# A recurrence and two dense layers on one core: chunk outputs as four products side by side with tokens on the partitions, turned by four transposes

## The chip, the cores and the metric

The kernel runs on one core of a Trainium2 chip. The metric is the device time of one launch in microseconds. An execution was profiled apart; its trace has every instruction of the five engines (PE is TensorE, DVE is VectorE, ACT is ScalarE, POOL is GpSimd, SP is SyncE) and the DMA packets.

## The reference

For 4 batches of 8 heads, each with a state of 40 x 40 numbers and 768 tokens, the attention part runs a recurrence; the result, 3072 tokens of 320 numbers, goes through two dense layers. All is in 32-bit floating point.

```python
for t in range(S):
    y[:, :, t] = np.einsum('bhd,bhde->bhe', rt, state)
    Sa = np.einsum('bhde,bhe->bhd', state, at)
    state_decay = state * wt[:, :, None, :] - np.einsum('bhd,bhe->bhde', Sa, bt)
    state = state_decay + np.einsum('bhd,bhe->bhde', vt, kt)
...
h = x @ w_in                      # 320 -> 1024
solu = h * softmax(h)
ln = (solu - mean) / sqrt(var + 1e-06) * g_ln
x = ln @ w_out                    # 1024 -> 320
...
h = x @ w_in                      # 320 -> 2048
g = np.maximum(h, 0.0) + alpha * np.minimum(h, 0.0)
out = g @ w_out                   # 2048 -> 320
```

## The kernel before

The 768 tokens are cut into 12 windows of 64 tokens, each of two chunks of 32, so there are 24 chunks. The 32 heads stand as 16 slots `s` times two groups `e`; a tile holds group 1 on its lower partitions and group 0 from partition 64 on. Within a chunk the recurrence is turned into matrix products and a triangular inverse; from chunk to chunk only the state goes on.

Chunk g has a time slot of its own, `slot(g)`, which records the stages of the recurrence in this order: `stage_x(g)` (tile `px`), `stage_uf(g-1)` (`pf`), `stage_u(g)` (`pu`), `stage_g2(g-1)` (`pg`, scores of a token against the chunk's tokens, masked by VectorE into `YS`), `stage_st(g)` (`pst`, the new state), `stage_y(g-1)` (`py`, the outputs of the chunk before), and `stage_s(g)` (`pss`, the state turned). Between them `side` puts transposes `pt` of coming windows (`trans`), products `pg` of `gen1`, and parts of the inverse (`pv`, `pn`). Into every gap the planner lets products of the first dense layers flow from a queue: `h` (line 803), `ptr`, `po` (line 877), `ptx`. After the last chunk come the last layers, `ph` (line 1324) and `acc` (lines 1342 to 1344).

The order on each engine is not written by hand: `note`, `pace`, `until` and `run` carry on a time of the planner's own, with a cost in microseconds for each step, and choose from it what stands next. Where the queue has nothing to give and the planner counts too few columns of late, `pop` puts a filler, a product of zeros called `zero` (line 313), or `busy` (line 358) in the first four slots. So other costs in one stage move instructions in every slot behind it.

The recurrence's products take their PSUM banks in turn from a ring of four (`bank`). A bank comes free when the engine that reads it is done (`ring[bk] = t + LAT`), and the fifth request waits for the first.

`stage_y` before: `blank(py)` (line 660) writes zeros into partitions 32 to 63 of the whole bank, 512 columns in bf16; then for each slot two products put 40 rows of `py` at partition 0 and 40 at partition 64, features on the partitions and 32 tokens on the free axis (line 750). VectorE multiplies all 104 partitions with H, the running product of the decays, into `Y` (line 756). Behind the second chunk of a window `x_move` sends `Y` to DRAM (`xd`), `x_load` brings it back, `x_split` makes `xt` of it (lines 784 to 788), and the first-layer products read that.

Of the kernel before, what the change touches and what calls it, by code (L numbers as in the profile page):

```python
# [18 lines left out]
D = 40  # L19
# [26 lines left out]
def tile_kernel(ctx: ExitStack, tc: tile.TileContext, w_fm, a0_fm, a_fm, kb_fm, r_fm, v_fm, v_tm,  # L46
# [66 lines left out]
    LMN = [lm.tile([128, 32, 32], F32, name=f"LMN{i}") for i in range(3)]  # L113
    VUS = [ca.tile([128, 2, 4, 2, 80], F32, name=f"VUS{i}") for i in range(2)]
    VUF = [ca.tile([120, 16, 2, 32], F32, name=f"VUF{i}") for i in range(2)]
    YS = [ca.tile([128, 2, 16, 32], F32, name=f"YS{i}") for i in range(2)]

    def f32(ap):
# [17 lines left out]
    def init():  # L136
        for t, c, k in ((GR, 0, 0), (VR, 0, 1), (LMN[2], 16, 2)):
            i = tri[:, 256 + 16 * k:272 + 16 * k].unsqueeze(1).to_broadcast([128, 32, 16])
            nc.gpsimd.tensor_copy(out=t[:, :, c:c + 16], in_=i)
        for t in YS:  # L140
            nc.gpsimd.memset(t[32:64, 1], 0.0)
            nc.gpsimd.memset(t[0:64, 0], 0.0)
            nc.gpsimd.memset(t[64:128, 1], 0.0)
        for t in VUS:
            nc.gpsimd.memset(t[32:64, 0], 0.0)
            nc.gpsimd.memset(t[32:64, 1], 0.0)
        for t in VUF:
            nc.gpsimd.memset(t[32:64], 0.0)
        for t in KBS:
            nc.gpsimd.memset(t[32:64, 0], 0.0)  # L150
            nc.gpsimd.memset(t[96:128, 1, 0], 0.0)
        for t, i in ((VUS[0], 0), (KBS[0], 1)):
            nc.gpsimd.memset(t[64:128, i], 0.0)
            nc.gpsimd.memset(t[0:32, 1 - i], 0.0)
        nc.gpsimd.memset(ebias, -float(896 << 23))
        nc.gpsimd.memset(half, -0.5)
        nc.gpsimd.memset(tiny, 1e-12)
        nc.gpsimd.memset(one, 1.0)
# [116 lines left out]
    def bank(shape, name):  # L275

        if not plain():
            until(lambda: ring[-4] if len(ring) > 3 else 0.0)
        ring.append(INF)
        return ps_at.tile(shape, F32, name=name, tag="at"), len(ring) - 1  # L280
# [79 lines left out]
    def flush(n):  # L360
        while len(queue) > n:
            if head():
                pop()
            else:
                until(queue[0][3])
# [289 lines left out]
            put(("U", g, pe))(t + LAT)  # L655
        ring[bk] = t + LAT

    def blank(p):

        nc.tensor.matmul(p[32:64].rearrange("p s t -> p (s t)"), lhsT=D1[:, 1:17].bitcast(BF16),  # L660
                         rhs=D1[:, 0:16 * p.shape[1]].bitcast(BF16), start=True, stop=True)
        note(0.11 * p.shape[1] / 8, 8 * p.shape[1], 1)

    def stage_uf(g):
        v, vuf = VUS[g % 2], VUF[g % 2]
        until(("U", g, 0), ("U", g, 1))
# [74 lines left out]
    def stage_y(g):  # L741
        w, c = divmod(g, 2)
        k, y = KBS[g % 4], YS[g % 2]
        until(("ys", g, 0), ("ys", g, 1), ("kb", g), ("ks", g))
        py, bk = bank([128, 16, 32], "py")
        blank(py)
        for s in range(16):
            for e, o in EO:
                K = 128 if e else 104 + s // 8 * 16
                nc.tensor.matmul(py[o:o + D, s, :], lhsT=k[0:K, 1 - e, s, :], rhs=y[0:K, e, s, :], start=True, stop=True)  # L750
            pace(0.08, 128, 4)
        ts = slice(c * 32, c * 32 + 32)
        if c == 0:
            st["Y"] = m1.tile([104, 16, 64], F32, name="Y")
        Y = st["Y"]
        t = run("V", 0.7, lambda: nc.vector.tensor_tensor(out=Y[:, :, ts], in0=py[0:104], in1=st[w]["H"][:, :, ts], op=ALU.mult),
                now[0] + PL)
        ring[bk] = t + LAT
        put(("yt", g))(t)
        if c and g < NG - 1:  # L760
            later(t, lambda: x_move(w))
# [398 lines left out]
    def slot(g):  # L1160
        st["slot"] = g
        fin = g == NG - 1
        queue.extend(mlp_tasks(g))
        box.setdefault("h", 0.0)
        nd = (ND if g < 4 else NL if g >= NG - 4 else NC)[g % 4]

        def due(n):
            lane["due"] += n
        if g + 1 < NG:
            load_v(g + 1)  # L1170
        stage_x(g)
        slot_tasks(g)
        side(g, "a")
        if g:
            stage_uf(g - 1)
        side(g, "b")
        stage_u(g)
        if g:
            stage_g2(g - 1, 0)
            stage_g2(g - 1, 1)  # L1180
        side(g, "c")
        due((nd + 3) // 4)
        if not fin:
            stage_st(g, 0)
            stage_st(g, 1)
        side(g, "x")
        due((nd + 1) // 4)
        if g == NG - 2:
            early_w()
        if g:  # L1190
            stage_y(g - 1)
        if g + 1 < NG:
            load_r(g + 1)
        side(g, "d")
        due((nd + 2) // 4)
        if not fin:
            stage_s(g)
        side(g, "e")
        due(nd // 4)
        side(g, "f")  # L1200
        flush(RES if g >= DEEP else MOST)
        side(g, "z")
        if fin:
            stage_uf(g)
            stage_g2(g, 0)
            stage_g2(g, 1)
            stage_y(g)
        flush(0 if fin else KQ if g >= DEEP else MOST)

    def phase1():  # L1210
# [484 lines left out]
```

## Time and profile before

| | |
|---|---|
| median of 3 runs | 1022.45 us (1016.11 to 1030.37) |
| profiled execution | 1025.12 us |
| its span, first to last instruction | 1023.1 us |
| mean granted clock of TensorE | 0.958 |
| busy: PE, DVE, ACT, POOL | 957.8, 658.2, 545.3, 302.4 us |

The span is what the trace covers; the execution's own time has 2.0 us around it. A busy PE is not a PE at its peak, since matmuls are pipelined and their ends are modelled: what a stage takes is best read from its first start to the first start of the stage behind it.

### The profile page before, as it was taken

Reading aid. Unit: us, or ns where it says so; the run is one execution under the profiler, and the core shown is the slowest. Engines: PE = TensorE matmul, PEld = TensorE weight load, DVE = VectorE, ACT = ScalarE, POOL = GpSimd, SP = SyncE. Lnnn points to the kernel's source line nnn. Section 1 sums busy time; section 2 is a strip of 40 time slices with the busy share of each in tenths; the row PEclk is TensorE's granted clock in tenths of the full one; section 3 lists DMA queues with packets and bytes.
Section 4 is the critical chain, followed back from the end, with each engine's and each line's share of the span. In section 5 each row is a group of like instructions: output and inputs, shape, how many; then the busy total and the mean of one; then the engine's idle time right before and its main releaser. Section 6 shows DMA issues by size and latency. Waiting matters only on the chain.

```text
span 1023.1 us, 34881 instructions
## 1 busy us (share of the span) xinstructions
PE 957.8 (94%) x15018; PEld 765.1 (75%) x15018; DVE 658.2 (64%) x1214; ACT 545.3 (53%) x1276; POOL 302.4 (30%) x352
## 2 busy tenths in 40 slices
PE   7789998999999999989999999899999999999996
PEld 3456566676677776767777767788989898989896
DVE  8797987688868886888864564634444445334443
ACT  1375657486768784858777785992121212212121
POOL 8500210113221221332121142623333333334332
PEclk8798977899899997999999999999999999999999
DMA  7634424333543353344353444442020100101010
GB/s 187 186 90 120 121 80 119 91 96 102 141 114 97 80 148 91 96 125 137 101 154 106 110 121 149 147 124 71 1 52 1 39 13 12 29 1 26 1 27 17
DMA packets 101532, 90.09 MB, mean 88 GB/s; under 512 B 52284, under 2 KB 76092, under 8 KB 101372
## 3 DMA queue, kind: packets, MB, share of 16 engines
q1 hardware_dynamic: 101372, 87.80, 31.1%
q8 instruction: 120, 1.97, 0.8%
q14 instruction: 40, 0.33, 0.1%
HBM read 70.20 MB, written 17.56 MB: 86 GB/s over the span
## 4 chain that ended last, share of the span: by engine, by line
PE 72%; ACT 12%; DVE 9%; issue 4%; DMA 1%; SPq 0%; POOL 0%; DVEq 0%; ACTq 0%; POOLq 0%
PE ph L1324 16%; PE po L877 9%; PE h L803 7%; PE acc L1342 5%; PE acc L1343 5%; PE acc L1344 5%; PE py L750 3%; PE pst L686 3%; ACT KBS L597 3%; PE pg L727 2%; PE pf L671 2%; PE pu L648 2%; PE pg L501 1%; PE zero L313 1%; PE pn L562 1%
## 5 line engine op out<-in xcount | busy, mean ns | idle before, releaser
L1331 POOL TENSOR_TENSOR gll<-gt,gh 128x512 fp32r<-128x512 f32 (+1 forms) x112 | 129.1, 1154 | 228.2 <-ACT gh L1330 222.3
L1330 ACT CAST gh<-gt 128x512 fp32r<-128x512 f32 (+1 forms) x112 | 62.5, 559 | 246.1 <-DVE gt L843 215.1
L842 DVE TENSOR_SCALAR gt<-ph,al 128x512 f32<-128x512 f32 (+1 forms) x112 | 75.4, 674 | 181.9 <-PE ph L1324 181.8
L877 PE MATMUL po<-wo,ln 128*128 128x320 f32 x384 | 131.1, 481 | 8.3 <-ACT ln L869 6.3
L877 PEld LDWEIGHTS po<-wo,ln 128*128 128x128 f32 x384 | 73.4, 204 | 36.3 <-ACT ln L869 7.1
L803 PE MATMUL h<-w1h,xt 128*128 128x512 f32 x240 | 90.2, 431 | 0.1
L1342 PE MATMUL acc<-w2h,gh 128*128 128x320 f32 x288 | 88.8, 308 | 0.0
L1343 PE MATMUL acc<-w2l,gh 128*128 128x320 f32 x288 | 88.8, 308 | 0.0
L1344 PE MATMUL acc<-w2h,gll 128*128 128x320 f32 x288 | 88.7, 308 | 0.0
L843 DVE SCALAR_TENSOR_TENSOR gt<-ph,gt 128x512 f32<-128x512 f32 (+1 forms) x112 | 68.6, 614 | 3.6
L735 DVE TENSOR_TENSOR YS<-pg,mask 64x256 f32<-64x256 f32 x96 | 40.4, 421 | 46.4 <-PE pg L727 44.7
L597 ACT COPY KBS<-pt 64x160 f32<-64x160 f32 x192 | 55.1, 287 | 18.4 <-PE pt L593 15.9
L803 PE MATMUL h<-w1l,xt 128*128 128x512 f32 x144 | 62.2, 432 | 0.2 <-POOL w1l L983 0.2
L822 POOL TENSOR_TENSOR sm<-sm,const 128x1 f32<-128x1 f32 x24 | 16.9, 704 | 151.4 <-ACT sm L819 141.0
L948 POOL TENSOR_TENSOR raw<-em 128x512 f32<-128x512 f32 (+1 forms) x28 | 36.0, 1292 | 85.7 <-issue 42.5
L1324 PE MATMUL ph<-w1h,w2h 128*128 128x512 f32 x180 | 59.3, 394 | 0.0
L358 PE MATMUL busy<-busy 128*128 128x512 bf16 x198 | 54.2, 422 | 1.3 <-POOL busy L1212 1.3
L1343 PEld LDWEIGHTS acc<-w2l,gh 128*128 128x128 f32 x288 | 54.1, 188 | 1.4
L1342 PEld LDWEIGHTS acc<-w2h,gh 128*128 128x128 f32 x288 | 54.1, 188 | 1.3
L1344 PEld LDWEIGHTS acc<-w2h,gll 128*128 128x128 f32 x288 | 54.1, 188 | 0.0
L512 ACT ACTIVATE GR<-pg 32x256 f32<-32x256 f32 x96 | 36.1, 376 | 31.2 <-PE pg L501 29.8
L712 ACT COPY KBS<-pss 40x320 f32<-40x320 f32 x92 | 38.7, 421 | 24.7 <-PE pss L709 23.4
(198 smaller groups left out, 2270.5 us busy)
## 6 DMA issues: line engine op xcount, KB each, us to landing
kbf<-in_kb_fm_dram SPq DMA_DIRECT2D x96, 96.0 KB
raw<-in_w_in_dram SPq DMA_DIRECT2D x14, 512.0 KB
raw<-in_w_out_dram SPq DMA_DIRECT2D x13, 512.0 KB
YS<-in_r_fm_dram SPq DMA_DIRECT2D x48, 112.0 KB
VUF<-in_v_fm_dram SPq DMA_DIRECT2D x48, 112.0 KB
wt<-in_w_fm_dram SPq DMA_DIRECT2D x24, 211.7 KB
VUS<-in_v_tm_dram SPq DMA_DIRECT2D x48, 80.0 KB
wr<-in_w_dram SPq DMA_DIRECT2D x8, 480.0 KB
```

The lines of the kernel that those rows point to most:

```text
L358: nc.tensor.matmul(st["busy"], lhsT=busy[:, 0:128], rhs=busy, start=True, stop=True)
L597: t = run("A", 0.29, lambda k=k, c=c, r=r, o=o: nc.scalar.copy(out=k[r:r + 64, 1 - r // 64, q * 4:q * 4 + 4, :], in_=pt[64 * c:64 * c + 64 ...
L803: nc.tensor.matmul(st["h"][:, ns], lhsT=l, rhs=r, start=j == 0, stop=j == len(ops) - 1)
L842: nc.vector.tensor_scalar(out=tmp, in0=h, scalar1=0.0, scalar2=al, op0=ALU.min, op1=ALU.mult)
L843: nc.vector.scalar_tensor_tensor(out=o, in0=h, scalar=0.0, in1=tmp, op0=ALU.max, op1=ALU.add)
L877: nc.tensor.matmul(po, lhsT=st["ln", t][:, piece], rhs=wo1[:, piece], start=piece == 0, stop=piece == K1 - 1)
L1324: nc.tensor.matmul(p, lhsT=l, rhs=r, start=j == 0, stop=j == len(ops) - 1)
L1330: nc.scalar.copy(out=gh, in_=t)
L1331: nc.gpsimd.tensor_tensor(out=gll, in0=t, in1=f32(gh), op=ALU.subtract)
L1342: nc.tensor.matmul(acc, lhsT=gh[:, cs], rhs=oh, start=f == 0, stop=False)
L1343: nc.tensor.matmul(acc, lhsT=gh[:, cs], rhs=ol, start=False, stop=False)
L1344: nc.tensor.matmul(acc, lhsT=gll[:, cs], rhs=oh, start=False, stop=f == K2 - 1)
```

## The change

The outputs are made the other way round: `YS` is the stationary operand (32 tokens) and the keys `KBS` the moving one (40 features). Four slots stand side by side on the 32-partition quarters of one bank, so that no partition is left unwritten, and the blanking product goes. ScalarE copies `py` into a new tile `YP`, whose features 40 to 63 were set to zero once at the start. A new stage, `stage_yt`, turns `YP` with four transposes into another bank of the ring, in the shape that `py` had before, and the product with H follows as it was. `stage_yt(g-1)` is recorded behind `stage_s(g)`, and for the last chunk right behind `stage_y`. The planner's cost of the products is 8 steps of 0.08 us in place of 16 and the blank; the transposes have 0.1 us each.

```diff
--- before.py
+++ after.py
@@ -113,6 +113,7 @@
     LMN = [lm.tile([128, 32, 32], F32, name=f"LMN{i}") for i in range(3)]
     VUS = [ca.tile([128, 2, 4, 2, 80], F32, name=f"VUS{i}") for i in range(2)]
     VUF = [ca.tile([120, 16, 2, 32], F32, name=f"VUF{i}") for i in range(2)]
+    YP = ca.tile([128, 4, 2, 64], F32, name="YP")
     YS = [ca.tile([128, 2, 16, 32], F32, name=f"YS{i}") for i in range(2)]
 
     def f32(ap):
@@ -137,6 +138,7 @@
         for t, c, k in ((GR, 0, 0), (VR, 0, 1), (LMN[2], 16, 2)):
             i = tri[:, 256 + 16 * k:272 + 16 * k].unsqueeze(1).to_broadcast([128, 32, 16])
             nc.gpsimd.tensor_copy(out=t[:, :, c:c + 16], in_=i)
+        nc.gpsimd.memset(YP, 0.0)
         for t in YS:
             nc.gpsimd.memset(t[32:64, 1], 0.0)
             nc.gpsimd.memset(t[0:64, 0], 0.0)
@@ -655,12 +657,6 @@
             put(("U", g, pe))(t + LAT)
         ring[bk] = t + LAT
 
-    def blank(p):
-
-        nc.tensor.matmul(p[32:64].rearrange("p s t -> p (s t)"), lhsT=D1[:, 1:17].bitcast(BF16),
-                         rhs=D1[:, 0:16 * p.shape[1]].bitcast(BF16), start=True, stop=True)
-        note(0.11 * p.shape[1] / 8, 8 * p.shape[1], 1)
-
     def stage_uf(g):
         v, vuf = VUS[g % 2], VUF[g % 2]
         until(("U", g, 0), ("U", g, 1))
@@ -742,13 +738,27 @@
         w, c = divmod(g, 2)
         k, y = KBS[g % 4], YS[g % 2]
         until(("ys", g, 0), ("ys", g, 1), ("kb", g), ("ks", g))
-        py, bk = bank([128, 16, 32], "py")
-        blank(py)
-        for s in range(16):
-            for e, o in EO:
-                K = 128 if e else 104 + s // 8 * 16
-                nc.tensor.matmul(py[o:o + D, s, :], lhsT=k[0:K, 1 - e, s, :], rhs=y[0:K, e, s, :], start=True, stop=True)
-            pace(0.08, 128, 4)
+        py, bk = bank([128, 4, 2, 40], "py")
+        for n in range(4):
+            for e in range(2):
+                for q in range(4):
+                    s = 4 * n + q
+                    K = 128 if e else 104 + s // 8 * 16
+                    nc.tensor.matmul(py[q * 32:q * 32 + 32, n, 1 - e, :], lhsT=y[0:K, e, s, :], rhs=k[0:K, 1 - e, s, :],
+                                     start=True, stop=True)
+                pace(0.08, 150, 8)
+        t = run("A", 0.43, lambda: nc.scalar.copy(out=YP[:, :, :, 0:D], in_=py), now[0] + PL)
+        ring[bk] = t + LAT
+        put(("YP", g))(t + LAT)
+
+    def stage_yt(g):
+        w, c = divmod(g, 2)
+        until(("YP", g))
+        py, bk = bank([128, 16, 32], "pyt")
+        for n in range(4):
+            nc.tensor.transpose(py[0:104, 4 * n:4 * n + 4, :].rearrange("p s t -> p (s t)"),
+                                YP[:, n].rearrange("p e d -> p (e d)")[:, 0:104], ident)
+            pace(0.1, 256, 1)
         ts = slice(c * 32, c * 32 + 32)
         if c == 0:
             st["Y"] = m1.tile([104, 16, 64], F32, name="Y")
@@ -1195,6 +1205,8 @@
         due((nd + 2) // 4)
         if not fin:
             stage_s(g)
+        if g:
+            stage_yt(g - 1)
         side(g, "e")
         due(nd // 4)
         side(g, "f")
@@ -1205,6 +1217,7 @@
             stage_g2(g, 0)
             stage_g2(g, 1)
             stage_y(g)
+            stage_yt(g)
         flush(0 if fin else KQ if g >= DEEP else MOST)
 
     def phase1():
```

In the order below, `L` numbers of the changed kernel are its own: 747 is the new output product, 759 the new transpose, 750 the new copy; `pss` is line 705, `pt` 595, `h` 813, `po` 887, `ptx` 901 there.

TensorE around the output of chunk 15, the second chunk of its window, before:

```order
L803 MATMUL h<-w1l,xt 128x512
L803 MATMUL h<-w1h,xt 128x512
L686 MATMUL pst<-VUS_170,KBS_158 40x40 x2
L660 LDWEIGHTS D_150
L660 MATMUL py<-D_150 32x512
L750 MATMUL py<-YS_175,KBS_161 40x32 x32
L593 MATMUL pt<-ident,kbf 128x104 x8
L709 MATMUL pss<-ident,VUS_171 120x40 x16
L593 MATMUL pt<-ident,kbf 128x104 x4
L803 MATMUL h<-w1h,xt 128x512
```

and now:

```order
L901 MATMUL ptx<-ident,xs 64x128
L813 MATMUL h<-w1h,xt 128x512
L747 MATMUL py<-KBS_161,YS_176 32x40 x32
L595 MATMUL pt<-ident,kbf 128x104 x8
L705 MATMUL pss<-ident,VUS_171 120x40 x16
L813 MATMUL h<-w1l,xt 128x512
L759 MATMUL pyt<-ident,YP 104x128 x4
L813 MATMUL h<-w1h,xt 128x512 x2
L813 MATMUL h<-w1l,xt 128x512
L595 MATMUL pt<-ident,kbf 128x104 x8
L813 MATMUL h<-w1h,xt 128x512
```

The blank is gone, a first-layer product stands between `pss` and the transposes, and the transposes stand between the two halves of the `pt` work.

ScalarE at the same chunk, from the copies of `ptx` to the copies of the turned state, before:

```order
L896 COPY x_7908<-ptx 64x128
L597 COPY KBS_160<-pt 64x160 x2
L597 COPY KBS_161<-pt 64x160 x2
L931 ACTIVATE em<-em,const 128x256
L932 ACTIVATE em<-em 128x256
L597 COPY KBS_160<-pt 64x160 x2
L597 COPY KBS_161<-pt 64x160 x2
L712 COPY KBS_159<-pss 40x320
L712 COPY KBS_159<-pss 56x320
L712 COPY KBS_159<-pss 40x320
L712 COPY KBS_159<-pss 56x320
```

and now:

```order
L906 COPY x_8002<-ptx 64x128
L849 ACTIVATE P<-P,sm 128x1024
L750 COPY YP<-py 128x8x40
L599 COPY KBS_160<-pt 64x160 x2
L599 COPY KBS_161<-pt 64x160 x2
L599 COPY KBS_160<-pt 64x160 x2
L599 COPY KBS_161<-pt 64x160 x2
L708 COPY KBS_159<-pss 40x320
L708 COPY KBS_159<-pss 56x320
L708 COPY KBS_159<-pss 40x320
L708 COPY KBS_159<-pss 56x320
```

The copy `YP` stands directly ahead of the copies of `pt` and `pss` into `KBS`; the decoding steps `em` are no longer among them.

TensorE at the last chunk, before:

```order
L313 LDWEIGHTS D_150
L313 MATMUL zero<-D_150 128x512
L660 LDWEIGHTS D_150
L660 MATMUL py<-D_150 32x512
L750 MATMUL py<-YS_175,KBS_161 40x32 x32
L891 MATMUL ptx<-ident,xs 128x128 x2
L891 MATMUL ptx<-ident,xs 64x128
L1324 MATMUL ph<-XS_10451,kbf 128x256 x6
```

and now:

```order
L723 MATMUL pg_11010<-YS_176,VUF_173 64x64 x16
L887 MATMUL po<-wo_148,ln 128x320 x4
L747 MATMUL py<-KBS_161,YS_176 32x40 x32
L887 MATMUL po<-wo_148,ln 128x320 x2
L759 MATMUL pyt<-ident,YP 104x128 x4
L901 MATMUL ptx<-ident,xs 128x128 x2
L901 MATMUL ptx<-ident,xs 64x128
L1337 MATMUL ph<-XS_10563,kbf 128x256 x6
```

The fillers ahead of the products are gone, and two products `po` stand between the products and the transposes, while ScalarE copies.

## Rows read from the trace of the kernel before

**Rows 1.** The page, part 1: busy time, share of the span, instructions.
```profile
PE 957.8 (94%) x15018; PEld 765.1 (75%) x15018; DVE 658.2 (64%) x1214; ACT 545.3 (53%) x1276; POOL 302.4 (30%) x352
```

**Rows 2.** The page, part 4: the chain by engine and by line.
```profile
PE 72%; ACT 12%; DVE 9%; issue 4%; DMA 1%; SPq 0%; POOL 0%; DVEq 0%; ACTq 0%; POOLq 0%
PE ph L1324 16%; PE po L877 9%; PE h L803 7%; PE acc L1342 5%; PE acc L1343 5%; PE acc L1344 5%; PE py L750 3%; PE pst L686 3%; ACT KBS L597 3%; PE pg L727 2%; PE pf L671 2%; PE pu L648 2%; PE pg L501 1%; PE zero L313 1%; PE pn L562 1%
```

**Rows 3.** Windows of two parts: start:end, length, busy us by engine, granted clock.
```profile
205.80:626.00 420.20, 397.00 (x9201) 303.83 (x9200) 313.56 (x626) 314.83 (x772) 102.83 (x142) 0.97 0.42 113
626.00:1023.00 397.00, 384.20 (x2213) 345.88 (x2209) 176.79 (x263) 126.90 (x247) 144.62 (x126) 1.00 0.15 44
```

**Rows 4.** Waits of matmuls: us in total, times, longest us.
```profile
PE po L877 <- ACT ln L869: 6.3, 4, 2.2
...
PE pss L709 <- ACT KBS L597: 3.2, 3, 2.0
```

**Rows 5.** Timeline around one chunk's output: start, us, instructions.
```profile
411.42 0.39 PE L660 MATMUL py<-D 104*32 104x512 bf16 x1
...
411.74 1.42 PE L750 MATMUL py<-YS,KBS 104*40 104x32 f32 x64
...
413.09 0.93 PE L593 MATMUL pt<-ident,kbf 104*128 104x104 f32 x8
...
413.23 0.69 DVE L756 TENSOR_TENSOR Y<-py,H 104x512 f32<-104x512 f32 x1 [0.21 <-PE py L750]
...
413.95 0.92 PE L709 MATMUL pss<-ident,VUS 40*120 40x40 f32 x16
```

**Rows 6.** Timeline around the stage `px` of another chunk.
```profile
534.89 0.80 PE L633 MATMUL px<-VUS,XS 104*32 104x40 f32 x64
...
535.62 0.44 PE L562 MATMUL pv<-VT,GR 16*32 16x16 f32 x32
...
535.99 3.50 PE L877 MATMUL po<-wo,ln 128*128 128x320 f32 x12
```

**Rows 7.** Groups by line and form, TensorE: busy us, mean ns, idle before.
```profile
L750 PE MATMUL py<-YS,KBS 128*40 128x32 f32 x768 | 35.2, 203 | 1.1 <-DVE YS L735 0.6 <-issue 0.4
L865 PE MATMUL ptr<-ident,P 128*128 128x128 f32 x192 | 34.0, 274 | 2.4 <-ACT P L839 2.4
...
L593 PE MATMUL pt<-ident,kbf 104*128 104x104 f32 x192 | 24.6, 261 | 2.3 <-DVE XS L521 0.9 <-ACT KBS L597 0.5 <-DVE VUS L691 0.5
...
L750 PE MATMUL py<-YS,KBS 104*40 104x32 f32 x384 | 20.1, 204 | 0.2 <-DVE YS L735 0.2
...
L633 PE MATMUL px<-VUS,XS 104*32 104x40 f32 x768 | 19.3, 206 | 3.3 <-issue 2.0 <-POOL VUS L153 1.3
```

**Rows 8.** Line 313, the filler: ns least/median/most, first and last start.
```profile
L313 PE MATMUL zero<-D x82: 377/379/650, 136.5 to 624.0; 104*128 104x512 bf16 x82
```

**Rows 9.** Timeline, same stretch as rows 5, where the clock is low.
```profile
394.89 0.28 PE L633 MATMUL px<-VUS,XS 104*32 104x40 f32 x8 [2.01 <-issue]
...
396.04 4.63 PE L877 MATMUL po<-wo,ln 128*128 128x320 f32 x8
...
408.50 0.60 PE L313 MATMUL zero<-D 104*128 104x512 bf16 x2
```

**Rows 10.** Groups by line and form, ScalarE.
```profile
L636 ACT COPY XP<-px 128x320 f32<-128x320 f32 x24 | 10.4, 433 | 3.4 <-PE px L633 3.2
```

**Rows 11.** Windows of 25 us, columns as in rows 3.
```profile
375.00:400.00 25.00, 21.44 (x467) 16.87 (x453) 18.78 (x37) 14.63 (x34) 6.08 (x8) 0.83 0.39 110
400.00:425.00 25.00, 24.21 (x478) 17.94 (x478) 17.64 (x48) 17.22 (x46) 2.87 (x6) 0.89 0.37 98
```

**Rows 12.** Timeline: a window's output on its way to the layers.
```profile
417.02 1.49 SPq L768 DMA_DIRECT2D xd<-Y  x4
...
433.81 0.42 DVE L788 TENSOR_TENSOR xt<-xraw,xt 64x256 fp32r<-64x256 f32 x1
...
434.79 0.48 PE L803 MATMUL h<-w1h,xt 128*128 128x512 f32 x1
...
435.11 0.39 PE L803 MATMUL h<-w1l,xt 128*128 128x512 f32 x1
```

## The prediction

> **What bounds the kernel now.** I read the page first, for the engines' shares and the chain that ended last; then the table by windows, to split the span into its two parts; then the timeline around one chunk, to price the stage that changes; then the groups by line for durations of the same operation elsewhere; then the waits, for what else could come to the front. The page shows TensorE busy 94% of the span, the next engine (VectorE) 64% [rows 1], and the chain of waits runs through TensorE for 72% of the time and through ScalarE for 12% [rows 2]. The windows show two parts: from 206 to 626 us, the recurrence with the first layers beside it, TensorE is busy 397.0 of 420.2 us at a granted clock of 0.97, and ScalarE 314.8; from 626 us to the end, the last layers, TensorE is busy nearly without a break and the change touches nothing [rows 3]. The largest waits of a matmul for another engine are 6.3 us in all of `po` for `ln` and 3.2 us of `pss` for ScalarE's copies [rows 4]. So in the middle stretch time taken from TensorE comes off the span almost one for one, until something else holds it. Ahead of 206 us this is not so: counted in the order, 46 of the 82 filler products `zero` stand ahead of the sixth chunk's output, so TensorE has time to fill there.
>
> **The output stage before.** In one ordinary chunk the blanking product starts at 411.42, the first output product at 411.74, and the next stage at 413.09 [rows 5]: 0.32 us for the blank and 1.35 us for 64 records (a matmul of 32-bit numbers leaves two records), 21 ns each, together 1.67 us. The blank's own row says 390 ns, but 0.32 us is what it holds up.
>
> **The output stage after, products.** They have the form of the stage `px` (four products side by side, 32 stationary columns, 40 moving). It starts at 534.89 and the stage behind it at 535.62 [rows 6]: 0.73 us for the same 64 records, 11 ns each. The rows by form give a single record of either stage 203 to 206 ns [rows 7], so the gain is overlap, not shorter records. The one thing that differs is that up to 128 rows are used here in place of 96 and 104; the output products of 104 and of 128 rows have the same mean today, 204 and 203 ns [rows 7]. I take 0.73 us; the other end is 1.35 us, no gain in overlap at all. The Trainium skill, "TensorE: Matmul & The Clock Gate", Part 1, in the section that asks "Wait — 56ns, not 53.3ns?", says that start-to-start never drops below about 25 ns however few columns a product has. By it the 64 records would need 1.6 us and this part would be a loss of 0.25 us a chunk; the trace does not agree, with 11 ns in `px` and 21 ns in `py`, both below that floor.
>
> **The output stage after, transposes.** Four a chunk, 128 rows, 128 moving columns. Eight transposes `pt` run from 413.09 to 413.95 [rows 5], 0.108 us each with the entry into the stage. The transposes `ptr` with 128 columns have a mean record of 274 ns against 261 ns of `pt` [rows 7], 5% more. Four cost 0.43 us; the bounds are 0.35 us (four fifths, where the tail runs under what follows) and 0.55 us (one more entry into a stage, as the blank's 0.32 us held one of about 0.1). So TensorE has 0.73 + 0.43 = 1.16 us in place of 1.67: **0.51 us less a chunk**, between +0.23 (products without overlap, dear transposes) and 0.59 less.
>
> **How many chunks count.** Five of the 24 outputs stand ahead of 206 us, where the order is stretched by waits; I give nothing for them. 19 remain: 19 x 0.51 = **9.7 us**. The last one has a new wait, products, ScalarE's copy, transposes; the order puts two products `po` between, and their 0.29 us each (twelve take 3.50 us, [rows 6]) cover the copy's 0.43 us, so I charge nothing. Without that cover it would be 0.4 us once.
>
> **What is given back.** (a) Fillers: the order has, by count, 89 `zero` in place of 82, and 195 products `busy` in place of 198. Behind the sixth output it is 49 in place of 36: 13 more. One takes 0.38 us by itself [rows 8], and two in a row 0.60 us [rows 9], so each further one adds 0.22: **2.8 us**. Between 0, if they stand where TensorE would have waited anyway, and 13 x 0.38 = 4.9 us. (b) ScalarE gets 24 copies `YP`, same size as `XP<-px`, 0.433 us each [rows 10]: 10.4 us. It is 75% busy in the middle stretch and carries 12% of the chain, so of 19 x 0.43 = 8.2 us I charge 15%, **1.2 us**; from 0 to 8.2. In the order it stands directly ahead of the copies of `pt` and `pss` into `KBS`, so these are late by 0.43 us, and what waits for them are the banks. (c) Banks: an output now takes two of the ring's four banks in turn, `py` freed by ScalarE in 0.43 us in place of VectorE's 0.69 [rows 5, 10], `pyt` by VectorE. Bank waits exist today, `pss` for ScalarE's copies three times and 3.2 us in all [rows 4]; I charge a third, **1.0 us**, from 0 to 3.2. (d) VectorE's product with H is the same instruction with the same size; nothing. (e) One memset at the start, on GpSimd, beside loading; nothing. (f) `YS` is freed as soon as the products end, which is now earlier; the memset and the loads of the next chunk behind it gain, but they are not late today.
>
> The sum: -9.7 + 2.8 + 1.2 + 1.0 = **-4.7 us**. The profiled execution took 1025.12 us and would take 1020.4; it stands 2.7 us above the median of the runs, so the forecast for a median is 1022.45 - 4.7 = 1017.8, rounded **1018 us**. With (a) to (c) at nothing and the transposes at 0.35 us the likeliest case is 19 x 0.59 = 11.2 us below the median, 1011 us; with (a) to (c) at their upper ends, 16.3 us together, it is 6.6 us above, 1029 us. The three runs of before lie 14 us apart, so a change of some 20 us (2%) is about what a measurement of this kernel can tell from no change.
>
> **Rivals.**
> Nothing arrives (0.22). The order is another one in every slot, and the freed half microsecond is spent in fillers, ScalarE's queue and bank waits: (a) and (b) at their upper ends, 4.9 + 8.2, would eat the 9.7 whole and 3.4 more. For it: the planner itself puts in 13 more fillers. Against it: TensorE's waits for others are small today [rows 4]. Time 1022 to 1026.
>
> The clock (0.13, to the fast side). The granted clock falls to the lower level, 1.2 GHz, in some stretches of the middle part; eight `po` records take 4.63 us there, 0.58 each [rows 9], where twelve take 3.50 us at 2.4 GHz, 0.29 each [rows 6], so a stretch costs half its length. The slice from 375 to 400 us has 0.83, the one from 400 to 425 has 0.89 [rows 11]. Over the whole middle part 0.97 is worth 420 x 0.03 = 12.6 us. Ahead of the slow `po` TensorE stood 2.01 us without a matmul, at the end of `px` [rows 9]. An order with more fillers and longer runs of transposes may avoid them all: 1018 - 12 = 1006 us. Against it: the new order has small products packed closer, after which the engine can also sit; so a part of this chance goes the other way, one such slice more being 25 x 0.17 = 4 us, within the range of the first case.
>
> The layers' input comes late (0.06, slower than before). `Y` is now written after the transposes, which stand behind `pss` and, in every second chunk, behind `pt` and a first-layer product too. In the piece of the order for chunk 15 that is 0.73 for the products, 0.86 for `pt`, 0.92 for `pss` [rows 5], 0.32 for a first-layer product (from one start to the next, [rows 12]) and 0.43, together 3.3 us from the start of the products against 1.67, 1.6 us later. Its readers are the DMAs `xd`, then the split `xt`, then the first-layer products. Where the input is the last to arrive, these start late: in one window `xt` ends at 434.23 and its first product starts at 434.79 [rows 12]. If all twelve windows had no slack it would be 12 x 1.6 = 19 us, 1018 + 19 = 1037 us; it undoes the gain from 0.4 us a window on. Against it: the DMA of `Y` was issued at 417.02, 3.1 us after VectorE had `Y` ready at 413.92 [rows 5, 12], held by what stands ahead on SyncE's queue, so 1.6 us are hidden in that window.
>
> The products don't overlap four by four (0.04, slower than before). They keep 1.35 us; 19 x 0.62 = 11.8 us more than forecast, 1030 us. It turns into a loss from 0.98 us a chunk on. What the Trainium skill's floor above would give lies at this end too. Against it is `px`, in every chunk.
>
> **How the numbers follow.** The first case has 0.55, the rivals 0.22, 0.13, 0.06 and 0.04. The likeliest is 1018. For 8 times in 10 the range takes the first two cases and most of the third: 1006 to 1030. Below 1002 us (2%) lies only the far end of the clock case with a low median, 0.08; above 1043 us only a late input that also costs clock, 0.04; within 2%, 0.88.
>
> **What would show it.** In the profile after: the products 0.73 us from start to next stage, right, or over 1 us, wrong; the four transposes 0.4 to 0.5 us; no blank; 24 copies of 0.43 us on ScalarE; TensorE's busy time in the middle part down by 7 to 10 us, and the start of the last layers (626 us) earlier by 5. If `pss` or `pt` wait for ScalarE by more than 3 us in all, (c) was too small. If first-layer products wait with `xt` as the releaser, the late input is it. If TensorE's records agree but the clock's mean in the middle part moved from 0.97, the clock decides, and not the stage. Wrong altogether would be a span that moves while the stage's own times don't.

## The result, and the profile after

The changed kernel takes 1010.02 us (median of 20 runs, 1004.86 to 1023.26), the kernel before 1022.77 us beside it (20 runs, 1014.37 to 1035.82). The ratio is 0.9891, with a 95% interval of [0.9862, 0.992]: 12.8 us at the medians, some 8 us more than forecast, and inside the range given. Medians and ranges take all runs, while ratios and the means of the table below leave out the slow ones, those over 1.5% above the fastest run of the same kernel (one of the 12 runs of `new_from_6` took 1731.23 us).

The stage itself came out as priced. The first view is the timeline of the changed kernel around one chunk's output (start, length in us, engine, line, operation, tiles, and in brackets idle time ahead):

```profile
390.23 0.81 PE L747 MATMUL py<-KBS,YS 104*32 104x40 f32 x64
...
390.97 0.93 PE L595 MATMUL pt<-ident,kbf 104*128 104x104 f32 x8
...
391.12 0.42 ACT L750 COPY YP<-py 128x320 f32<-128x320 f32 x1 [0.95 <-PE py L747]
...
391.93 0.90 PE L705 MATMUL pss<-ident,VUS 40*120 40x40 f32 x16
...
394.29 0.60 PE L759 MATMUL pyt<-ident,YP 128*104 128x128 f32 x4
...
394.65 0.71 PE L813 MATMUL h<-w1h,xt 128*128 128x512 f32 x2
...
395.37 0.69 DVE L766 TENSOR_TENSOR Y<-pyt,H 104x512 f32<-104x512 f32 x1
```

The products hold TensorE from 390.23 to 390.97, 0.74 us, and the transposes from 394.29 to 394.65, 0.36 us: together 1.10 us, in place of the 0.32 + 1.35 us of [rows 5]. Over the 24 chunks the products take 0.74 us in all but seven, where the instructions come with gaps (0.83 to 1.35), and the transposes 0.35 to 0.58, but for the last chunk, where they take 0.60 and 0.51 us of waiting stand behind them. The groups by line say the same (busy us, mean ns of one):

```profile
L315 PE MATMUL zero<-D 104*128 104x512 bf16 x89 | 25.0, 400 | 0.0
...
L747 PE MATMUL py<-KBS,YS 128*32 128x40 f32 (+2 forms) x1536 | 20.7, 202 | 0.6 <-issue 0.3 <-DVE YS L731 0.3
...
L759 PE MATMUL pyt<-ident,YP 128*104 128x128 f32 x96 | 15.3, 282 | 0.0
```

The page, part 1 (answers to [rows 1]), and the windows of the changed kernel, cut at the seventh chunk's first product and at the last layers (answers to [rows 3]; columns: start:end, length, busy us of PE, PEld, DVE, ACT, POOL, granted clock, DMA share, GB/s):

```profile
PE 937.1 (93%) x15094; PEld 752.9 (75%) x15094; DVE 657.6 (65%) x1214; ACT 553.7 (55%) x1300; POOL 304.0 (30%) x353
```
```profile
0.00:188.90 188.90, 163.70 (x3558) 107.50 (x3560) 165.94 (x323) 103.43 (x259) 56.20 (x86) 0.90 0.49 131
188.90:606.00 417.10, 390.08 (x9336) 299.66 (x9335) 315.41 (x630) 323.23 (x794) 103.76 (x141) 0.98 0.43 115
606.00:1006.30 400.30, 383.30 (x2208) 345.75 (x2206) 176.20 (x262) 127.01 (x248) 144.02 (x126) 0.99 0.15 43
```

TensorE is busy 20.7 us less in all [rows 1], and in the middle part 6.9 us less than in [rows 3], where 7 to 10 were forecast. But the length of that part hardly follows. The same cuts in the kernel before:

```profile
0.00:205.80 205.80, 176.56 (x3614) 115.40 (x3615) 167.84 (x325) 103.56 (x258) 54.91 (x85) 0.86 0.45 123
134.60:162.80 28.20, 27.83 (x578) 20.09 (x577) 22.02 (x42) 17.18 (x45) 3.27 (x6) 0.76 0.31 79
162.80:205.80 43.00, 38.28 (x718) 25.16 (x718) 28.31 (x51) 21.90 (x50) 4.90 (x7) 0.76 0.33 96
```

So in this pair of profiles the stretch ahead of the seventh chunk became 16.9 us shorter (205.8 to 188.9), and, cut at the first product of the last layers (626.84 before, 605.96 after), the middle part 3.9 us shorter (421.0 to 417.1) and the last layers 4.0 us longer (396.3 to 400.3). Of the part ahead, the fifth and the sixth chunk's slots (from one chunk's first `px` to the next one's) are all: 28.2 + 43.0 us in the rows above, and in the changed kernel

```profile
137.50:160.60 23.10, 22.11 (x579) 16.55 (x575) 22.32 (x46) 18.00 (x48) 3.92 (x6) 1.00 0.36 84
160.60:188.90 28.30, 26.00 (x651) 18.30 (x652) 25.96 (x45) 20.08 (x45) 5.36 (x7) 1.00 0.47 132
```

19.8 us less, at a granted clock of 1.00 in place of 0.76. The timeline of the kernel before shows what fills its sixth slot:

```profile
164.22 0.62 PE L671 MATMUL pf<-ident,VUS 32*120 32x32 f32 x8
167.08 1.44 PE L877 MATMUL po<-wo,ln 128*128 128x320 f32 x2 [2.23 <-ACT ln L869]
...
187.43 4.28 PE L313 MATMUL zero<-D 104*128 104x512 bf16 x19
193.34 1.14 PE L877 MATMUL po<-wo,ln 128*128 128x320 f32 x2 [1.63 <-DVE wo L945]
```

A wait of 2.23 us for ScalarE's `ln`, behind it a stretch at 1.2 GHz (166.4 to 180.0 by the clock's records), then 19 fillers in a row and 1.63 us of waiting for weights that VectorE decodes, and again 1.2 GHz (193.7 to 200.5). The changed kernel makes the same eight output products of this tile; in its order `ln` is there in time, and the weights are there 11 us earlier, 9 us of it counted from the slot's start:

```profile
162.88 1.88 PE L887 MATMUL po<-wo,ln 128*128 128x320 f32 x6
...
181.95 1.34 PE L887 MATMUL po<-wo,ln 128*128 128x320 f32 x4 [1.02 <-DVE wo L955]
```

None of this is the stage that was changed. So there were two theories, which the first expectations call A and B. **S**: TensorE's time per chunk, 0.51 us less, comes off the span (A). **O**: the planner, given other costs and another stage, writes another order, and that order, not the stage, is faster (B).

### The profile page after: what moved, and what is told of

Read it like the earlier page. It is cut to its first block, busy times and chain, and to the rows that moved or that the text cites. A ratio compares the mean times of both kernels' runs of the same rounds, so it can differ in the third digit from the quotient of the medians.

```text
span 1006.3 us, 35061 instructions
## 1 busy us (share of the span) xinstructions
PE 937.1 (93%) x15094; PEld 752.9 (75%) x15094; DVE 657.6 (65%) x1214; ACT 553.7 (55%) x1300; POOL 304.0 (30%) x353
## 4 chain that ended last, share of the span: by engine, by line
PE 61%; ACT 9%; issue 3%; DMA 1%; POOL 1%; DVE 1%; SPq 0%; POOLq 0%; DVEq 0%; ACTq 0%
PE ph L1337 16%; PE po L887 8%; PE acc L1355 5%; PE acc L1356 5%; PE acc L1357 5%; PE h L813 5%; PE pst L682 2%; PE pg L723 2%; PE ptr L875 2%; ACT KBS L599 2%; PE pf L667 1%; PE pu L650 1%; PE pn L564 1%; ACT P L849 1%; ACT wo L1378 1%
## 5 line engine op out<-in xcount | busy, mean ns | idle before, releaser
L887 PE MATMUL po<-wo,ln 128*128 128x320 f32 x384 | 124.4, 466 | 2.4 <-ACT ln L879 1.4
L360 PE MATMUL busy<-busy 128*128 128x512 bf16 x195 | 57.3, 448 | 1.3 <-POOL busy L1225 1.3
L621 POOL MEMSET YS<- 64x512 f32 x44 | 24.3, 553 | 91.9 <-PE py L747 90.7
L396 POOL MEMSET XS<- 32x512 f32 (+1 forms) x36 | 18.7, 519 | 110.5 <-PE px L635 109.5
```

The source lines that it names most:

```text
L360: nc.tensor.matmul(st["busy"], lhsT=busy[:, 0:128], rhs=busy, start=True, stop=True)
L887: nc.tensor.matmul(po, lhsT=st["ln", t][:, piece], rhs=wo1[:, piece], start=piece == 0, stop=piece == K1 - 1)
```

## The experiments

All ratios are to the kernel before, run on the same chip. Two columns of the table further down are worked out from every run's time and mean granted clock: "clock" is (1 - clock) x time, an estimate of what the lower level costs where TensorE sets the pace (half of each stretch spent at it), and "rest" is the time less that. The runs of one and the same kernel say that it is too large by a quarter to a third: over those of the kernel before, the time falls by 7.5 to 8.1 us for each 0.01 of clock (lines through its runs beside each of three sets of experiments), where the estimate says 10.2.

**Second profiles** (`before_2`, `after_2`)**.** Both kernels, unchanged.

> The kernel before, profiled a second time, to see what repeats. Theory B (the order and with it the clock pays, ahead of 206 us above all): the sixth chunk's slot again takes about 43 us, from its first product px to the next chunk's, and TensorE's granted clock in the two slots before 206 us is again about 0.76. Theory A (each chunk's stage pays in its place): that slot's length is an accident of one execution, and comes out nearer to 30 us here, with the span some 10 us shorter.

> The changed kernel, profiled a second time. Theory B: the fifth and sixth chunks' slots again take about 51 us together, at a granted clock near 1.0. Theory A: they may come out at 51 to 71 us, as the clock falls, and the stretch from the seventh chunk to the last layers is again 4 us shorter than before's 421.

Measured 1021.41 and 1011.09 us. The slots repeat to a fraction: 28.2 and 43.0 us at 0.76 before, 23.2 and 28.8 us at 1.00 after.

```profile
137.50:165.70 28.20, 27.84 (x579) 20.07 (x581) 22.04 (x42) 17.19 (x45) 3.28 (x6) 0.76 0.33 86
165.70:208.70 43.00, 38.23 (x717) 25.19 (x717) 28.27 (x51) 21.84 (x50) 4.93 (x7) 0.76 0.31 92
208.70:623.40 414.70, 395.49 (x9203) 302.87 (x9202) 313.90 (x627) 314.70 (x773) 101.96 (x143) 0.98 0.42 114
```
```profile
141.30:164.50 23.20, 22.21 (x581) 16.56 (x577) 22.39 (x46) 18.08 (x48) 3.90 (x6) 1.00 0.36 83
164.50:193.30 28.80, 25.83 (x651) 18.21 (x653) 25.93 (x45) 19.84 (x45) 5.38 (x7) 1.00 0.47 130
193.30:608.80 415.50, 387.62 (x9334) 298.66 (x9334) 315.29 (x630) 323.44 (x794) 103.37 (x141) 0.98 0.42 116
```

The middle part is 414.7 us before and 415.5 us after: the gain of the first pair, 4 us in it, was not the stage, while TensorE is busy 7.9 us less. As mean of the two pairs the part ahead is 16.2 us shorter, the middle 1.5 us, the last layers 4.2 us longer. In the first pair 2.2 of the 4.0 us lost there lie ahead of the last product's end, where TensorE waits longer, most of all for ScalarE's `P` (3.9 us in place of 1.7), and 1.8 lie behind it:

```profile
PE ptr L875 <- ACT P L849: 3.9, 4, 2.9
PE ptx L901 <- ACT xs L890: 2.2, 1, 2.2
```

**The new order with the old work** (`plan_after_work_before`)**.** The changed kernel's order and plan; blank and 64 two-group products in place of the new ones, no transposes, no copy; the bank of the transposes is taken and not used.

```diff
-        py, bk = bank([128, 4, 2, 40], "py")
+        py, bk = bank([128, 16, 32], "py")
+        blank(py)
...
+            for s in (2 * n, 2 * n + 1):
+                for e, o in EO:
...
+                    nc.tensor.matmul(py[o:o + D, s, :], lhsT=k[0:K, 1 - e, s, :], rhs=y[0:K, e, s, :], ...)
-        t = run("A", 0.43, lambda: nc.scalar.copy(out=YP[:, :, :, 0:D], in_=py), now[0] + PL)
+        t = run("A", 0.43, lambda: None, now[0] + PL)
...
-            nc.tensor.transpose(py[0:104, 4 * n:4 * n + 4, :] ...)
```

> The order of the changed kernel, its fillers included, but TensorE's work at the chunk's output is that of before: blank, 64 products in two groups, no transposes, no copy on ScalarE. Theory A (TensorE's time per chunk pays): 0.51 us x 24 = 12 us go back on TensorE, so the time is that of before, 1022 us, ratio to before 1.00. Theory B (the order pays): the time is that of the changed kernel, 1010 us, ratio 0.988.

1008.09 us, ratio 0.9883 [0.9822, 0.9943]: the whole gain, without the new stage. TensorE's instructions stand in the changed kernel's order throughout, its 89 fillers included. The middle part:

```profile
191.50:602.00 410.50, 391.14 (x9277) 301.71 (x9277) 315.89 (x629) 316.18 (x775) 104.35 (x141) 0.99 0.43 116
```

Theory S is refuted as it stands, unless ScalarE's copy, which is left out here too, had made up for the 12 us. So the same with a copy of equal size, read by nobody (`order_new_copy_too`):

```diff
-        t = run("A", 0.43, lambda: None, now[0] + PL)
+        t = run("A", 0.43, lambda: nc.scalar.copy(out=YP[0:104] ..., in_=py[0:104] ...[:, 0:320]), now[0] + PL)
```

> As plan_after_work_before (the order of the changed kernel, TensorE's work of before), and ScalarE makes a copy of the same 320 columns per chunk at the changed kernel's place, which nobody reads. So against the changed kernel only TensorE's own work differs, 0.51 us more in each of 24 chunks. Theory S: 6 to 12 us more than the changed kernel, 1016 to 1022 us, since the copy left out hid it in plan_after_work_before. Theory O: within 3 us of the changed kernel, 1007 to 1013 us.

1007.17 us, 0.983 [0.9784, 0.9875]. 0.51 us more of TensorE per chunk, 12 us in all, cost nothing that can be measured; the two intervals are 12 and 9 us wide. Its middle part:

```profile
193.40:608.20 414.80, 393.53 (x9279) 303.43 (x9278) 316.20 (x629) 323.50 (x794) 104.34 (x141) 0.99 0.42 115
```

TensorE is busy 393.5 us here and 390.1 and 387.6 us in the changed kernel's two profiles, and the part is as long, 414.8 against 417.1 and 415.5: what the stage saves is idle there. The last layers take 396.5 and 396.9 us in these two kernels, as before, so that within this order the 4 us lost there came with the new stage.

**The old costs with the new work** (`plan_before_work_after`)**.** The planner books before's costs, which was to give before's order and fillers, while TensorE makes the new products and, behind the next stage, the transposes, in the same bank; ScalarE copies.

```diff
...
+        note(0.22, 128, 1)
...
-                pace(0.08, 150, 8)
+                for _ in range(2):
+                    pace(0.08, 128, 4)
-        t = run("A", 0.43, lambda: nc.scalar.copy(out=YP[:, :, :, 0:D], in_=py), now[0] + PL)
+        nc.scalar.copy(out=YP[:, :, :, 0:D], in_=py)
+        t = run("V", 0.7, lambda: None, now[0] + PL)
...
```

> The order of before, with its fillers and its planned costs, but TensorE and ScalarE do the new work at the chunk's output: products four side by side, ScalarE's copy, and the four transposes behind the next stage, in the same bank. Theory S (the stage's TensorE time pays): 12 us less, about 1011 to 1014 us. Theory O (the new order pays, by the clock and the waits ahead of 206 us): the sixth chunk's slot stays at about 43 us, and the time at 1018 to 1022 us.

1022.67 us, 0.9972 [0.9936, 1.0009]: no gain. The sixth slot took 34.8 us and not 43, so that half of O's expectation missed. But the order is not before's. From 173 us on TensorE's instructions stand in another sequence, and there are 95 fillers, 50 of them in the middle part, where the kernel before has 82 and 38:

```profile
L315 PE MATMUL zero<-D 104*128 104x512 bf16 x95 | 26.3, 399 | 0.5 <-issue 0.5
```

So this is the new work in one more order, and no run has it in before's. Nor does the plan know of the copy: the transposes wait 4.7 us for it, and `pss` for ScalarE 8.5 us in place of the 3.2 us of [rows 4]:

```profile
PE pss L705 <- ACT KBS L599: 8.5, 11, 2.0
...
PE py L762 <- ACT YP L753: 4.7, 2, 2.8
```

**The new stage for some chunks only** (`new_until_6`, `new_from_6`)**.** Chunks 0 to 5 with the new output and 6 to 23 with the old one, and the other way round.

```diff
...
-            stage_y(g - 1)
+            (stage_y if g - 1 < 6 else stage_y_old)(g - 1)
...
-        if g:
+        if g and g - 1 < 6:
             stage_yt(g - 1)
```

> The new output stage for the first six chunks alone, the one of before for the other 18. Theory S: a quarter of the 12 us, about 1019 us. Theory O: the stretch ahead of 206 us is the changed kernel's, the fifth and sixth slots together 51 us in place of 71, and all of the 12 us or more are there: 1007 to 1013 us.

> The other way round: the stage of before for the first six chunks, the new one for the other 18. Theory S: three quarters of the 12 us, about 1013 us; by the prediction's own sum (19 chunks, gain less what is given back) 1018 us. Theory O: the sixth slot stays at 43 us, and the time is 1018 to 1022 us.

New until 6: 1000.14 us, 0.9772 [0.9719, 0.9825], faster than either kernel, with only a quarter of the stages new. New from 6: 1018.85 us, 0.9927 [0.989, 0.9965]. The first has the changed kernel's sixth slot and yet another order behind it, the second keeps a long one (38.4 us, at a clock of 0.91):

```profile
163.50:192.50 29.00, 25.77 (x647) 18.18 (x646) 25.89 (x45) 19.83 (x45) 5.37 (x7) 1.00 0.47 128
...
192.50:596.70 404.20, 388.80 (x9271) 300.53 (x9271) 308.91 (x623) 314.04 (x773) 98.30 (x138) 0.99 0.43 117
```
```profile
163.30:201.70 38.40, 33.30 (x718) 22.36 (x719) 28.46 (x51) 21.88 (x50) 5.07 (x7) 0.91 0.36 104
201.70:621.60 419.90, 388.62 (x9265) 298.81 (x9264) 309.88 (x625) 321.81 (x788) 106.28 (x140) 0.97 0.42 113
```

The 18 new stages of the second are in a middle part of 419.9 us, the 18 old ones of the first in one of 404.2. What the second gains in its profile lies ahead of the middle part (201.7 us against 205.8 and 208.7), where its work and TensorE's order are before's and the clock of the two slots is higher.

**Another order with nothing else** (`before_replanned`)**.** The kernel before, and the planner books 0.10 us more for the output stage (0.02 for the blank, 16 x 0.005 for the products; the expectation says 0.12); the work is the same, the order and the fillers are not.

```diff
-        note(0.11 * p.shape[1] / 8, 8 * p.shape[1], 1)
+        note(0.12 * p.shape[1] / 8, 8 * p.shape[1], 1)
...
-            pace(0.08, 128, 4)
+            pace(0.085, 128, 4)
```

> The kernel before, same work, and the planner books the output stage 0.12 us longer (blank 0.24 for 0.22, each pair of products 0.085 for 0.08), which gives it another order. If the order of before was simply an unlucky one ahead of 206 us, any other may be better: 1005 to 1020 us. If it takes the new stage's shorter work to get the better order: 1020 to 1026 us.

1005.82 us, 0.9808 [0.9761, 0.9855]. A wrong number in the plan brings more than the change. And it comes elsewhere: the fifth and sixth slots are before's to a tenth (28.1, 43.1 at 0.76), and the middle part is 402.2 us.

```profile
138.00:166.10 28.10, 27.73 (x573) 20.00 (x570) 21.97 (x41) 17.10 (x45) 3.29 (x6) 0.76 0.33 86
166.10:209.20 43.10, 38.13 (x713) 25.11 (x712) 28.40 (x52) 21.93 (x50) 4.94 (x7) 0.76 0.32 92
209.20:611.40 402.20, 387.75 (x9199) 298.99 (x9199) 312.18 (x627) 314.04 (x772) 100.51 (x141) 0.99 0.43 116
```

So theory O holds, but not in the form that I gave it: the two slots are where this order wins, they are not what an order must win.

**The clock in before's sixth slot** (`before_fill`)**.** Idle products ahead of the two waits.

```diff
+        if t == 0 and piece in (0, 6):
+            z, k = (po, 160) if piece == 0 else (st["z"][0], 256)
+            for _ in range(12 if piece == 0 else 7):
+                nc.tensor.matmul(z, lhsT=D1[:, 1:65].bitcast(BF16), rhs=D1[:, 0:k].bitcast(BF16), ...)
         nc.tensor.matmul(po, lhsT=st["ln", t][:, piece], rhs=wo1[:, piece], ...)
```

> The kernel before, its order untouched, with 12 idle products of 320 columns ahead of the first and 7 of 512 ahead of the seventh output-layer product of the first tile, where TensorE stood 2.23 us for ScalarE's ln and 1.63 us for VectorE's weights. They are written where nobody reads, and the planner doesn't know of them. Theory C (TensorE's clock in the sixth slot is what the new order wins): the clock stays at 1.0 there, the slot goes from 43 us to 33 us and the time from 1023 to about 1013 us. If the clock falls all the same, or only the waits themselves count (their 3.9 us stay as long as before): 1021 to 1025 us.

1018.56 us, 0.9946 [0.9914, 0.9979], half of what was expected. The first group did not fill its gap, since by the trace it waited for ScalarE's `ln` itself:

```profile
166.24 2.42 PE L880 MATMUL po<-D 104*128 104x320 bf16 x12 [2.16 <-ACT ln L869]
168.46 1.27 PE L881 MATMUL po<-wo,ln 128*128 128x320 f32 x2
```

The sixth slot took 39.4 us at 0.96, 3.6 us less than before; what parts it from the changed kernel's 28.3 us is its waits and fillers, 1.6 us of clock aside. The fifth took 22.9 us at 1.00, with nothing changed in it: as short as the changed kernel's 23.1, so that those 5 us need no new order. By the table, the gain of this kernel is all clock, and the rest is what it was.

**The cost of the stage's parts in the changed order.** The blank put back ahead of the new products, unknown to the planner (`blank_back`):

```diff
-        py, bk = bank([128, 4, 2, 40], "py")
+        p_, bk = bank([128, 512], "py")
+        blank(p_)
+        py = p_[:, 0:320].rearrange("p (n e d) -> p n e d", n=4, e=2)
```

> The changed kernel in its own order, and the blanking product (512 columns) back ahead of the products, written where they write afterwards, not known to the planner. Theory S (TensorE's time in the stage pays): 24 x 0.32 = 7.7 us more, about 1018 us. Theory O (in the middle stretch what TensorE saves becomes idle time): at most 2 us more, 1008 to 1013 us.

1006.86 us, 0.9837 [0.9794, 0.988]. No cost that can be measured. It was a weaker test than meant: blank and products took 0.92 us from start to next stage in most chunks, where the products alone take 0.74, so 4.3 us in all and not 7.7.

```profile
395.32 0.39 PE L662 MATMUL py<-D 104*32 104x512 bf16 x1
395.33 0.99 PE L754 MATMUL py<-KBS,YS 104*32 104x40 f32 x64
396.25 0.93 PE L595 MATMUL pt<-ident,kbf 104*128 104x104 f32 x8
```

ScalarE's copy left out (`after_no_copy`), so that the transposes turn zeros:

```diff
-        t = run("A", 0.43, lambda: nc.scalar.copy(out=YP[:, :, :, 0:D], in_=py), now[0] + PL)
+        t = run("A", 0.43, lambda: None, now[0] + PL)
```

> The changed kernel in its own order, and ScalarE's copy left out: the transposes turn a buffer of zeros, so Y is zero and the output is not the reference's. If the 10.1 us of copies and the waits that hang on them (pt for YP 1.9 us, the copies of pt and pss behind it) are what ate the gain of the middle stretch: that stretch 4 to 8 us shorter, 1002 to 1006 us. If they are covered: 1008 to 1011 us.

1009.34 us, 0.9838 [0.9782, 0.9895], an interval that overlaps the change's own. The middle part, where the gain was looked for, is as long as with the copy, which is covered there:

```profile
189.20:606.50 417.30, 390.42 (x9336) 300.87 (x9335) 315.67 (x630) 316.40 (x775) 103.44 (x141) 0.97 0.43 115
```

Last, four products in a row to the same 32 partitions (`serial_groups`):

```diff
-                for q in range(4):
-                    s = 4 * n + q
+                for m in range(4):
+                    s = 4 * m + n
...
-                    nc.tensor.matmul(py[q * 32:q * 32 + 32, n, 1 - e, :], ...)
+                    nc.tensor.matmul(py[n * 32:n * 32 + 32, m, 1 - e, :], ...)
```

> The changed kernel, with the same products, but four in a row go to the same 32 partitions of the output in place of four different ones. If the gain is that four groups work side by side, the stage goes from 0.74 us to 1.35 us or more (one group at a time, at 53 ns a product, would be 1.7 us), so 24 x 0.6 to 1.0 = 15 to 23 us more than the changed kernel, 1025 to 1033 us. If the products are short because of their form alone, the stage stays at 0.74 us and the time at 1010 us.

1026.17 us, 1.0048 [1.0016, 1.008]. The stage goes to 2.09 us (65 ns a product, where the expectation took 53), so the four groups side by side are what makes it short, and 24 x 1.35 = 32.4 us more of TensorE cost 16 us: this much is no longer covered, and still half of it is.

```profile
399.22 2.15 PE L747 MATMUL py<-KBS,YS 104*32 104x40 f32 x64
401.31 0.93 PE L595 MATMUL pt<-ident,kbf 104*128 104x104 f32 x8
```

The means over the runs, in us:

| kernel | order | output stage | time | clock | rest |
|---|---|---|---|---|---|
| before (49 runs, beside the experiments) | before's | old | 1023.4 | 41.3 | 982.1 |
| `plan_before_work_after` (11) | a sixth | new | 1022.1 | 40.1 | 982.1 |
| `before_fill` (12) | before's | old | 1018.6 | 35.4 | 983.2 |
| `new_from_6` (11) | before's, then a third | old, then new | 1017.4 | 38.8 | 978.6 |
| `before_replanned` (6) | a fourth | old | 1005.8 | 33.7 | 972.1 |
| after (18) | after's | new | 1010.5 | 35.4 | 975.1 |
| `plan_after_work_before` (6) | after's | old | 1007.0 | 32.2 | 974.8 |
| `order_new_copy_too` (6) | after's | old, and a copy | 1007.4 | 29.1 | 978.3 |
| `blank_back` (6) | after's | new, and the blank | 1007.7 | 32.1 | 975.6 |
| `after_no_copy` (5) | after's | new, no copy | 1008.0 | 35.5 | 972.5 |
| `new_until_6` (6) | after's, then a fifth | new, then old | 1001.5 | 28.7 | 972.8 |
| `serial_groups` (10) | after's | new, one quarter at a time | 1025.8 | 31.0 | 994.8 |

Within the changed kernel's order the stage moves the time only where it grows by 32 us; between orders the same work lies up to 18 us apart (the kernel before against `before_replanned`). Between before and after, 5.9 of the 12.9 us are clock by this estimate (some 4 by the slope of the runs), and 7.0 are the rest.

## Why the prediction was right, and for what reason it wasn't

The sign held, and the time lies inside the range, 8 us from the likeliest value. The mechanism that was to bring it did not hold: what was gained came from the order, not from the stage, so that the range held is luck.

- **Products 0.73 us**: right, 0.74. The four-way overlap is real, and `serial_groups` shows it from the other side. The rival that it doesn't come is out.
- **Transposes 0.43 us**: right, 0.35 to 0.60, with a mean of 0.45 over the last 19 chunks, the wait behind the last one left out. That one wait was charged nothing: the two products `po` ahead of the transposes cover the copy, though the 0.29 us taken for each is the length of a record, and they are two records each and took 1.18 us. The mean record of 282 ns stands beside the 274 ns of `ptr` [rows 7].
- **"Time taken from TensorE comes off the span almost one for one"**: this is the step that failed. I read 397.0 busy of 420.2 us [rows 3] as a limit. But 38 fillers are in that busy time, and 23.2 us are idle: at 0.22 us a filler, some 32 us in which TensorE has nothing that it must do. What the stage frees goes there: in the middle part the changed kernel is idle 27.0 and 27.9 us (length less busy) against 23.2 and 19.2, and has 49 fillers. That is 6.2 us more of the one and, at 0.22 us each, 2.4 of the other, 8.7 together, beside some 9 us freed (from start to start the 19 stages there took 32.5 us before and 23.4 after). With the fillers alike it is seen best: in the same order with the old work TensorE is idle 19.4 us (`plan_after_work_before`) and 21.3 (`order_new_copy_too`). `order_new_copy_too` puts 0.51 us a chunk back and `blank_back` 0.18 us, at no cost that can be measured.
- **What is given back, -4.7 in place of -9.7**: (a) had the right count (13 more fillers behind the sixth output, 11 counted from the seventh chunk's first product). (b) and (c), 2.2 us, were far too small if they are to stand for the idle time, and they named the wrong cause: without the copy the middle part is 417.3 us, as long as with it. The new idle time hangs on no single wait. In the middle part of the changed kernel the longest are

```profile
PE pu L650 <- issue: 4.6, 4, 1.8
PE pn L564 <- issue: 3.1, 2, 1.7
PE pf L667 <- ACT XP L638: 2.9, 1, 2.9
PE ptx L901 <- ACT xs L890: 2.7, 5, 0.7
```

- **"Five of the 24 outputs stand ahead of 206 us; I give nothing for them"**: as to the stage that may be right, but the stretch as a whole was left out of the sum, and it is where the change won 16.2 us (mean of two pairs). The order there was another one, and I had looked only at what the stage does in it.
- **The rivals.** "Nothing arrives" described the middle part: 1.5 us. "The clock" had the right kind of gain and the wrong place: the middle part went from 0.97 and 0.98 to 0.98 and 0.98, the part ahead of the seventh chunk from 0.86 and 0.84 to 0.90 and 0.89, which by (1 - clock) x length is 29 and 34 us before, 19 and 20 us after. A late layers' input is not in the waits: no first-layer product waits for `xt`.
- **"Wrong altogether would be a span that moves while the stage's own times don't."** `plan_after_work_before` and `before_replanned` are just that.

What is shown: the new order, with the old work, gives the gain, and in the new order the stage's parts can be changed by 4 to 12 us of TensorE at no cost that intervals of 9 to 12 us let see. Not shown is what the new work would bring in before's order, which no run has. What stays open is why one order is better than another. In this pair the fifth and sixth slots carry it, in `before_replanned` the middle part does, with those slots as they were. The two shortest middle parts, of `before_replanned` and `new_until_6`, have the least idle time of TensorE, 14.5 and 15.4 us, and a clock of 0.99; a common cause behind that was not found. That a filled gap alone keeps the clock up could not be settled either: the slot's clock fell for a shorter time in `before_fill` (0.96), but `new_from_6`, with no filler added, had 0.91 in its sixth slot and 1.00 in its fifth, where both profiles of before, with the same products in the same sequence, show 0.76.

## What to carry to other kernels

Where a planner lays out the order, a change of one stage is two changes, and the second can be the larger: here 0.10 us too much booked for one stage moved the time by 2%, the stage, in the changed kernel's order, by nothing that can be measured. Run the new order with the old work, and the old work with a slightly wrong plan, and compare the instruction orders in the traces, before a stage's saving is believed or a good change thrown away. And a busy share is no proof of a bound: take off the fillers, add the idle time, and compare this slack with what the change is to save.

## What the runs showed of the hardware

- Products that write different quarters of the 128 output partitions in turn follow each other faster than products in a row to the same quarter: 64 records of 32 columns by 40 take 0.74 us with the four quarters in turn, 11 ns from start to start, 1.35 us with two groups in turn (40 columns by 32) [rows 5], 21 ns, and 2.09 us four in a row in one quarter, 33 ns. The Trainium skill's lowest start-to-start of about 25 ns ("TensorE: Matmul & The Clock Gate", Part 1, in the section that asks "Wait — 56ns, not 53.3ns?") lies between them; the trace does not agree with it for the first two. Counted by product, of two records each, it is 23, 42 and 65 ns, and only the first is below.
- The overlap holds for unlike products too. The blank of 512 columns, which writes one quarter, costs 0.32 us ahead of the old products [rows 5] and 0.18 us ahead of the new ones, whose first record starts 0.01 us behind it.
- The mean granted clock is not a property of the program: over 16 runs of the kernel before it lay between 0.952 and 0.970, and the time between 1030.5 and 1017.0 us, 7.7 us for each 0.01. A line through them takes up two thirds of the spread (squared deviations) of this kernel's times.
